# Gate, up and query projections with x held and the weights streamed, in a decode kernel on one core

## The chip, the cores and the metric

One NeuronCore of a Trainium2 chip runs the whole kernel. The metric is the device time of one execution in microseconds (us). Its five instruction queues are PE (TensorE; matmuls, with weight loads shown apart as PEld), DVE (VectorE), ACT (ScalarE), POOL (GpSimd) and SP (SyncE, which here issues every DMA). Matmuls write to PSUM, which is 8 banks of 128 partitions x 512 float32 values.

## What is computed

Two layers, each an attention block over a long cache and then a gated feed-forward, for a batch of 4 with one new token each (D = 512, 32 query heads, 8 key heads, 8192 cached positions, head size 128, F = 1792, all bfloat16). The same weights and caches serve both layers.

```python
def _A_ref(x, k_cache, v_cache, wq, wo):       # k_cache, v_cache: [4, 8, 8192, 128]
    q = (x @ wq).reshape(B, Sq, Hq, Dh).transpose(0, 2, 1, 3)
    k = jnp.repeat(k_cache, rep, axis=1)       # rep = 4
    v = jnp.repeat(v_cache, rep, axis=1)
    scores = jnp.einsum("bhqd,bhkd->bhqk", q, k) * (Dh ** -0.5)
    p = _softmax(scores, axis=-1)
    o = jnp.einsum("bhqk,bhkd->bhqd", p, v)
    return o.transpose(0, 2, 1, 3).reshape(B, Sq, Hq * Dh) @ wo

def _B_ref(x, w_gate, w_up, w_down):
    return (_silu(x @ w_gate) * (x @ w_up)) @ w_down

x = A_x
x = x + _A_ref(_layernorm(x), ...); x = x + _B_ref(_layernorm(x), ...)
x = x + _A_ref(_layernorm(x), ...); x = x + _B_ref(_layernorm(x), ...)
```

The caches are 128 MiB in all and are read almost wholly twice; that is nearly all the kernel's traffic.

## The kernel before

**Units.** The work is cut into 16 units, each a pair of key heads (`gp`, 0 to 3) and a batch element (`b`). A unit's K and its V are 4 MiB each. Layer 0 takes the units from 0 to 15, layer 1 takes 15, 14, 13, 12 and then 0 to 11, so that what lies in SBUF at the end of layer 0 can be used again.

**Slots and loads.** SBUF has four slots of 4 MiB and a fifth, `QS`, which first holds `wq`. The list `cmds` fixes the order of all loads: K and V of the units, the four parts of `wo`, at each layer's end the weights of the feed-forward (`W`: gate, up and the first parts of down; `W+`, `Wp`, `W0` to `W2`: the other parts of down). `pump` issues the next load on SP as soon as its place is free; `freed`, called as the program is written out, marks a place as free, and the issue then waits on semaphores for the last reader. Late in layer 1 a load is issued some 40 us before it lands.

**Scores and values.** K arrives with positions in partitions. VectorE transposes it in place, 32x32 blocks of 4-byte pairs (`turn`, L558). `scores` (L582) multiplies by `zq`, a stationary operand in which the unit's scaled queries stand in otherwise zero columns; GpSimd fills it for each unit from `qr` (`place_q`, L572), and VectorE does so for the first unit of a layer. The maximum of a unit (L588, L593, L596), the exponentials (L629), the transposes of the weights into `pT` (L646) and the products with V (`values`, L718, four 32-column quarters of the array at once) follow as an order written out by hand: `blocks` is the queue of PE work, `line` a queue of small steps that are let in between. The results of a unit are gathered (L766, L770), summed over partitions (L775) and scaled into `oT` (L780).

**After a group of heads.** When the four units of a `gp` are done, `close_group` lets `mix` (L801, L805) regroup the heads of `oT` so that they suit the layout of `wo`, and `rows` (L836) or, for the last group, `project` (L861) multiplies by `wo`. In both layers `mix` runs for the first two groups together, for the third and for the fourth by itself.

**Layer norm.** `center` (L884 to L898) subtracts the mean and squares; `deviation` (L903 to L907) gets 1/sqrt(variance) as `rstd`, which is multiplied in after the projection.

**Queries.** `qproj` (L917) holds 128x128 pieces of `wq` and moves the 4 columns of `xn`: 4 row blocks of D times 32 heads, 128 matmuls. The result has the head's 128 elements in partitions. VectorE multiplies by `rstd` into `qT` (L926), 16 matmuls with pieces of the identity (L936) spread it over partitions in the order that `scores` needs, and VectorE writes the first unit's `zq` (L572) and the copy `qr` for the others (L941). In layer 1 each eighth of `wq` is freed after its last matmul, for K.

**Feed-forward.** `ffn` (L961) does gate and up in the same way: 14 columns of F times 4 row blocks of D, 56 matmuls each. After the first, second and third row block of gate, places are freed for the last parts of down in layer 0. `rstd` is asked for after the second row block. Then come silu and the product (L975 to L982) into `hT`. The down projection is L999 in layer 0, with the weights held; in layer 1 `hT` is held and the weights move, in four quarters (L989). The final steps are two copies on VectorE (L1064) and two on ScalarE (L1062) and one store. Between the last matmuls of attention in layer 1 stand some matmuls that only keep PE busy (`stream`, L698). Two parts of `x_rows` (L879) add x itself into the result.

**The weights' layout.** With weights held, a piece of 128 columns is read with a stride of 2 or 4 (`columns`, `base`), because `w_down` lies in SBUF so that a partition holds `e` neighbouring rows of it; the third number in `WDS` is `e`.

## Time and profile before

| | us |
|---|---|
| median of 3 runs (644.95 to 645.78) | 645.25 |
| the profiled execution | 645.21 |
| its span, first to last instruction | 643.4 |

| engine | busy us | share of the span | instructions |
|---|---|---|---|
| PE matmuls | 416.7 | 65% | 3126 |
| PE weight loads | 180.0 | 28% | 3128 |
| VectorE | 421.7 | 66% | 593 |
| ScalarE | 42.3 | 7% | 118 |
| GpSimd | 11.6 | 2% | 44 |

271.8 MB pass the DMA engines at a mean of 422 GB/s. The mean granted clock of TensorE is 0.83 of full speed; it changes between 1.0 and 0.5 many times. The parts that the change touches:

| group | count | busy us | mean ns of one |
|---|---|---|---|
| L917 queries, matmul 128x4 | 256 | 7.5 | 166 |
| L961 gate and up, matmul 128x4 | 224 | 7.0 | 168 |
| L936 spreading the queries, matmul | 32 | 0.8 | 241 |
| L801 mix, matmul | 96 | 2.5 | 208 |
| L926, L941 queries on VectorE | 4 | 1.4 | 353 |
| L975 to L982 silu and product on VectorE and ScalarE | 14 | 3.6 | 258 |

Matmuls overlap in the array, so the busy time of a group is less than its count times the mean. "Idle before, releaser" in a row names what the engine waited for. Line numbers (L961) are those of the kernel before.

### The profile page before, as it was taken

What the parts mean: (1) busy time and instruction counts of PE and PEld (TensorE: products, weight loads), DVE (VectorE), ACT (ScalarE), POOL (GpSimd) and SP (SyncE); (2) the same over time, 40 slices, a digit from 0 to 9 for tenths busy, and PEclk for the clock granted to TensorE, in tenths of its full rate; (3) what the DMA queues carried; (4) which work ended last, traced back from release to release, by engine and by line L of the source; (5) the groups of instructions that cost most, each with busy time, mean ns of one, the idle gap of its engine ahead of it and who ended that gap; (6) DMA issues with size and microseconds to landing.
All of it is one profiled execution on the core that took longest, in us unless ns stands there. A gap on an engine that the chain in (4) does not pass through costs nothing.

```text
span 643.4 us, 7434 instructions
## 1 busy us (share of the span) xinstructions
PE 416.7 (65%) x3126; PEld 180.0 (28%) x3128; DVE 421.7 (66%) x593; ACT 42.3 (7%) x118; POOL 11.6 (2%) x44
## 2 busy tenths in 40 slices
PE   0673376456765757757866977776555577557877
PEld 0421122112222322222226432332221232222324
DVE  5275467455776656776952688887765567755964
ACT  0000000000000000000010110000000000000110
POOL 0000000000000000000000000000000000000000
PEclk9995786698877889766975899999778887769877
DMA  9999999999999999999999999999999999999996
GB/s 372 442 424 416 430 444 426 431 424 429 438 436 423 428 433 439 426 426 431 440 406 380 416 431 431 436 429 425 432 435 432 427 430 438 429 428 429 440 408 257
DMA packets 15872, 271.79 MB, mean 422 GB/s; under 512 B 1624, under 2 KB 1632, under 8 KB 7264
## 3 DMA queue, kind: packets, MB, share of 16 engines
q1 hardware_dynamic: 15840, 271.33, 99.0%
q8 instruction: 24, 0.39, 0.2%
q14 instruction: 8, 0.07, 0.0%
HBM read 271.32 MB, written 0.00 MB: 422 GB/s over the span
## 4 chain that ended last, share of the span: by engine, by line
DMA 61%; DVE 19%; PE 15%; issue 3%; another core or an unknown queue 1%; SPq 0%; DVEq 0%
DMA kvf<-in_A_k_cache_dram 49%; DVE kvf L558 15%; DMA kvf<-in_A_v_cache_dram 11%; PE ps L582 9%; PE ps L718 2%; DVE pb L770 2%; DMA kvf<-in_B_w_down_dram 1%; PE ps L961 1%; PE ps L917 1%; DVE pb L766 0%; DVE pT L646 0%; DVE scr L780 0%; SPq L93 0%; PE ps L861 0%
## 5 line engine op out<-in xcount | busy, mean ns | idle before, releaser
L582 PE MATMUL ps<-kvf,zq 128*128 128x512 bf16 x1024 | 292.9, 432 | 183.5 <-DVE kvf L558 178.8
L558 DVE STREAM_TRANSPOSE kvf<-kvf 128x2048 f32<-128x2048 f32 (+1 forms) x133 | 280.5, 2132 | 128.4 <-DMA kvf<-in_A_k_cache_dram 128.0
L582 PEld LDWEIGHTS ps<-kvf,zq 128*128 128x128 bf16 x1024 | 99.1, 108 | 340.2 <-DVE kvf L558 222.6
L718 PE MATMUL ps<-kvf,pT 128*32 128x512 bf16 x960 | 67.6, 405 | 1.1 <-DVE pT L646 1.1
L629 ACT ACTIVATE pb<-ps,tiny 128x512 bf16<-128x512 f32 x32 | 22.0, 687 | 525.9 <-DVE tiny L627 505.1
L646 DVE STREAM_TRANSPOSE pT<-pb 64x512 bf16<-64x512 bf16 x60 | 41.2, 686 | 2.7 <-ACT pb L629 1.7
L770 DVE SCALAR_TENSOR_TENSOR pb<-ps,tiny,pb 128x128 f32<-128x128 f32 x104 | 36.5, 351 | 4.7 <-PE ps L718 0.8
L588 DVE TENSOR_REDUCE tiny<-ps 128x1 f32<-128x512 f32 x32 | 22.0, 687 | 20.1 <-PE ps L582 20.1
L718 PEld LDWEIGHTS ps<-kvf,pT 128*32 128x32 bf16 x960 | 21.0, 99 | 31.2 <-issue 16.0
L775 PEld LDWEIGHTS ps<-sel,pb 128*128 128x128 f32 x64 | 17.0, 273 | 16.5 <-DVE pb L770 8.3
L572 POOL TENSOR_TENSOR zq<-scr,tiny 128x64 bf16<-128x64 bf16 x30 | 9.0, 299 | 527.1 <-PE ps L582 527.1
L596 DVE TENSOR_REDUCE mrm<-ps 1x8 f32<-1x128 f32 x32 | 8.8, 275 | 13.6 <-PE ps L593 13.6
L775 PE MATMUL ps<-sel,pb 128*128 128x8 f32 x64 | 12.4, 267 | 5.8 <-DVE pb L770 5.8
L619 PEld LDWEIGHTS ps<-mrm,tiny 128*128 128x128 f32 x60 | 13.0, 223 | 9.2 <-DVE scr L780 3.2
L917 PE MATMUL ps<-xn,kvf 128*128 128x4 bf16 x256 | 7.5, 166 | 11.5 <-DMA kvf<-in_A_wq_dram 11.2
L766 DVE TENSOR_SCALAR pb<-ps,tiny 128x128 f32<-128x128 f32 x32 | 10.1, 315 | 3.0 <-PE ps L718 3.0
L619 PE MATMUL ps<-mrm,tiny 128*128 128x16 f32 x60 | 9.9, 241 | 3.1 <-ACT mrm L631 3.1
L836 PE MATMUL ps<-wo_sb,scr 128*4 128x512 bf16 x48 | 11.0, 379 | 0.5 <-DVE scr L805 0.5
L917 PEld LDWEIGHTS ps<-xn,kvf 128*128 128x128 bf16 x256 | 7.3, 105 | 11.8 <-DMA kvf<-in_A_wq_dram 11.4
L631 ACT ACTIVATE mrm<-head,tiny 128x8 f32<-128x8 f32 x32 | 9.6, 301 | 1.0
L593 PE MATMUL ps<-identf,tiny 128*1 128x128 f32 x32 | 8.7, 273 | 0.7 <-DVE tiny L588 0.7
L790 DVE TENSOR_TENSOR xT<-xT,ps 128x16 f32<-128x16 f32 x6 | 1.0, 171 | 10.4 <-PE ps L846 4.7
(87 smaller groups left out, 120.3 us busy)
## 6 DMA issues: line engine op xcount, KB each, us to landing
kvf<-in_A_k_cache_dram SPq DMA_DIRECT2D x27, 4096.0 KB, 31.2
kvf<-in_A_v_cache_dram SPq DMA_DIRECT2D x27, 4096.0 KB, 33.9
kvf<-in_A_v_cache_dram SPq DMA_DIRECT2D x3, 2048.0 KB, 25.2
kvf<-in_A_k_cache_dram SPq DMA_DIRECT2D x9, 512.0 KB, 7.9
kvf<-in_A_k_cache_dram SPq DMA_DIRECT2D x2, 2048.0 KB, 9.4
kvf<-in_A_wq_dram SPq DMA_DIRECT2D x2, 2048.0 KB, 18.1
wo_sb<-in_A_wo_dram SPq DMA_DIRECT2D x4, 1024.0 KB, 41.4
kvf<-in_B_w_gate_dram SPq DMA_DIRECT2D x2, 1792.0 KB, 23.9
```

The costliest lines, as they stand in the source:

```text
L558: T.op("dve", lambda e: e.transpose(w, w), reads=names, writes=names)
L582: T.op("pe", lambda e: e.matmul(bank(bk)[:, 0:SW], lhsT=zq[:, z0:z0 + P], rhs=w[:, :, c // 2, :, c % 2], start=(q == 0 and c == 0), stop=( ...
L588: T.op("dve", lambda e: e.tensor_reduce(mx[:], bank(bk)[:, 0:SW], AX.X, ALU.max), reads=[f"pb{bk}"], writes=["mx"])
L619: T.op("pe", lambda e: e.matmul(at, lhsT=ones, rhs=mrm[:, i * H2:(i + 2) * H2], start=True, stop=True), reads=[f"m8{i}", "rsm", "onesf"], ...
L629: T.op("act", lambda e: e.activation(pb[:], bank(bk)[:, 0:SW], ACTF.Exp, bias=nm, accum_out=rs), reads=[f"pb{bk}", "nm"], writes=PB + ["rs"])
L646: T.op("dve", lambda e: e.transpose(dst, pb[hp]), reads=["pb", "row"], writes=[name])
L718: T.op("pe", lambda e: e.matmul(bank(k)[j * QB:(j + 1) * QB, q0 * Dh:q1 * Dh], lhsT=p_t[:, t, h, :], rhs=v[:, q0:q1, t, :], start=((last o ...
L766: T.op("dve", lambda e: e.tensor_scalar(into, o, own[:, q:q + 1], None, op0=ALU.mult), reads=[f"pb{k}", "own"], writes=["row"] if last els ...
L770: T.op("dve", lambda e: e.scalar_tensor_tensor(into, o, own[:, q:q + 1], into, op0=ALU.mult, op1=ALU.add), reads=[f"pb{k}", "own", iname], ...
L775: T.op("pe", lambda e: e.matmul(at, lhsT=into, rhs=sel[:], start=True, stop=True), reads=[iname, "sel"], writes=[name])
L836: T.op("pe", lambda e: e.matmul(bank(OUTB)[0:B, 0:D], lhsT=oT[:, h, :], rhs=wo_sb[:, h, :], start=(gp == groups[L][0] and r == 0), stop=(g ...
L917: T.op("pe", lambda e: e.matmul(at[:, h * B:(h + 1) * B], lhsT=wq_sb[:, kt, h * Dh:(h + 1) * Dh], rhs=xn[:, kt * B:(kt + 1) * B], start=(k ...
```

## The change

`qproj`, gate and up now hold the 4 columns of `xn` and move the weights. The output of a matmul is 4 partitions (the batch) by up to 512 columns. Four such matmuls, for four strips of columns, go to the four 32-column quarters of the array and so to partitions 0 to 3, 32 to 35, 64 to 67 and 96 to 99 of one bank. Gate and up have strips of 448 columns (`FW`), 16 matmuls each, and one strip of up is cut in two where its weights lie in two places. The queries have eight strips of 512 columns in two banks, 32 matmuls.

VectorE then transposes the bank in 32x32 blocks (`on_end`), which brings the columns back into partitions. For gate and up it is one transpose of 448 in place each, ahead of the same silu and product, whose operands now have the batch outside. Since a partition then holds 14 neighbouring rows of F, `w_down` is loaded so that each partition has 14 neighbouring rows too; in layer 1 its first two parts are runs of 8 and 4 KB instead of 2 KB.

For the queries there are two transposes of 512. In layer 0 both come before the first unit's `zq` is filled, in layer 1 only one of them does. `zq` is filled by two scaled copies on VectorE and two on ScalarE. Eight multiplications by `rstd`, of 32 partitions each, write `qr`. The 16 spreading matmuls, `qT` and L926, L936 and L941 go.

Two banks of PSUM are cleared once at the start, as the transposes read partitions that no matmul writes.

`mix` of layer 1 now takes the first three groups at once (`spot` gives a group's place in `oT` by its turn); in layer 0 it stays as it was. `deviation` uses another spare bank in `qproj`.

By the order of the instructions, no DMA issue changes its place on SP.

```diff
-        WDS = (((12, 14, 2), (10, 12, 2), (0, 2, 2), (2, 6, 4), (6, 10, 4)), ((0, 8, 2), (8, 12, 2), (12, 14, 2)))
+        WDS = (((12, 14), (10, 12), (0, 2), (2, 6), (6, 10)), ((0, 8), (8, 12), (12, 14)))
...
+        def wg_at(s, k, f, n):
+            o = s * SL + k * F + f
+            return kvf[:, o:o + n]
+
+        def wu_at(s, k, f, n):
             o = k * F + f
-            return columns((NSLOT + 1) * SL + o if o < RES else s * SL + O_WU + o - RES, e)
+            o = (NSLOT + 1) * SL + o if o < RES else s * SL + O_WU + o - RES
+            return kvf[:, o:o + n]
+
+        def strips(up, k):
+            for a in range(NA):
+                cuts = [a * FW, (a + 1) * FW]
+                if up and cuts[0] < RES - k * F < cuts[1]:
+                    cuts.insert(1, RES - k * F)
+                for f, end in zip(cuts, cuts[1:]):
+                    yield a, f, end - f
...
+        T.op("dve", lambda e: e.memset(ps[:, SBK[1] * BANKF:(OBK[0] + 1) * BANKF], 0.0),
+             writes=[f"pb{SBK[1]}", f"pb{OBK[0]}"])
...
+            a, b = WDS[L][j]
             o = 0 if w0 is pTf else wd_from(L, a)
-            T.dma("sp", w0[:, o:o + (b - a) * D].rearrange("p (m x) -> p m x", x=e_ * D),
-                  B_w_down[a * P:b * P, :].rearrange("(m p e) n -> p m (e n)", p=P, e=e_), sem_w["wd"][j],
+            T.dma("sp", w0[:, o:o + (b - a) * D], B_w_down.rearrange("(p f) n -> p (f n)", f=FO)[:, a * D:b * D], sem_w["wd"][j],
...
+            n = spot(L, gp)
+            if n < (1, 2)[L]:
                 return
-            gs = [0, 1] if gp == 1 else [gp]
-            line.append([0.5, None, lambda: mix(gs, fill)])
+            gs = groups[L][:n + 1] if n == (1, 2)[L] else [gp]
+            line.append([0.5, None, lambda: mix(L, gs, fill)])
...
+            gp, b = pair_gb(u)
+            first = gp // 2
+            W2 = REP * Dh
+            QK = (SBK[1], OBK[0])
+            assert W2 == BANKF and GP == 4 and QK[1] == QK[0] + 1
             for kt in range(KT):
                 if kt == KT // 2:
-                    deviation(lsc_sb, "lsc")
-                for h in range(Hq):
-                    q, last = 2 * kt + h * 2 // Hq, (h + 1) * 2 % Hq == 0
-                    T.op("pe", lambda e: e.matmul(at[:, h * B:(h + 1) * B],
-                                                  lhsT=wq_sb[:, kt, h * Dh:(h + 1) * Dh],
-                                                  rhs=xn[:, kt * B:(kt + 1) * B],
-                                                  start=(kt == 0 and h == 0), stop=(kt == KT - 1 and h == Hq - 1)),
-                         reads=[WQ[q], "xn"], writes=[name], sig=last)
-                    if L and last and q < NB - 2:
+                    deviation(lsc_sb, "lsc", SBK[0])
+                for k in ((first, 1 - first) if kt == KT - 1 else (0, 1)):
+                    q = 2 * kt + k
+                    for a in range(NA):
+                        f = ((2 * k + a % 2) * 2 + a // 2) * W2
+                        T.op("pe", lambda e: e.matmul(bank(QK[k])[a * QB:a * QB + B, :],
+                                                      lhsT=xn[:, kt * B:(kt + 1) * B], rhs=wq_sb[:, kt, f:f + W2], start=(kt == 0), stop=(kt == KT - 1)),
+                             reads=[WQ[q], "xn"], writes=[f"pb{QK[k]}"], sig=(a == NA - 1))
+                    if L and q < NB - 2:
                         if q == NB - 3:
                             T._wait("act", T._need((), [WQ[q]]))
                         freed(QS, q, q + 1)
-            T.op("dve", lambda e: e.tensor_tensor(qT, at.rearrange("p (h b) -> p b h", b=B),
-                                                  rstd[:].unsqueeze(2).to_broadcast([P, B, Hq]), ALU.mult),
-                 reads=[name, "rstd"], writes=["qT"] + OT)
-
-            pick = ident.rearrange("p (c j e) -> p c j e", c=2, e=2)
-            ob, oname = place("q", 0, NQR)
-            ob = ob.rearrange("p (c b g r) -> p c b g r", c=4, b=B, g=GP)
-            qv = qT.rearrange("p b (g h r) -> p b g h r", h=2, r=REP)
-            for c in range(4):
+
+            TO = (OBK[0], ONE)
+            assert TO[1] == TO[0] + 1 and TO[0] == QK[1]
+            ends = ps[:, TO[0] * BANKF:(TO[1] + 1) * BANKF].rearrange("p (k i r c) -> p k i r c", k=2, i=QB, r=REP)
+
+            def on_end(k):
+                src = bank(QK[k]).rearrange("p (x i e) -> p x e i", i=QB, e=2)
+                dst = bank(TO[k]).rearrange("p (i x e) -> p x e i", i=QB, e=2)
+                T.op("dve", lambda e: e.transpose(dst, src), reads=[f"pb{QK[k]}"], writes=[f"pb{TO[k]}"])
+
+            def place_first():
+                placed_q.add((L, u))
                 for a in range(NA):
-                    T.op("pe", lambda e: e.matmul(ob[a * QB:(a + 1) * QB, c],
-                                                  lhsT=pick[:, c // 2, :, c % 2],
-                                                  rhs=qv[:, :, :, a // 2, :], start=True, stop=True),
-                         reads=["qT", "ident"], writes=[oname], sig=(a == NA - 1))
-            place_q(L, u, "dve", ob, [oname])
-            T.op("dve", lambda e: e.tensor_copy(qr, ob), reads=[oname], writes=["qr", "made"])
+                    to = slice(a * QB, (a + 1) * QB)
+                    g = a // 2 * 2 + gp % 2
+                    of = slice(g * QB, (g + 1) * QB)
+                    dst = zd[to, :, a, 0:REP].rearrange("p c r -> p r c")
+                    src = ends[of, first, b]
+                    if a // 2:
+                        T.op("act", lambda e: e.activation(dst, src, ACTF.Copy, scale=rstd[of, b:b + 1]),
+                             reads=[f"pb{TO[first]}", "rstd"], writes=["zq1"])
+                    else:
+                        T.op("dve", lambda e: e.tensor_scalar(dst, src, rstd[of, b:b + 1], None, op0=ALU.mult),
+                             reads=[f"pb{TO[first]}", "rstd"], writes=["zq"])
+
+            on_end(1)
+            if first:
+                place_first()
+            on_end(0)
+            if not first:
+                place_first()
+            for a in range(NA):
+                to = slice(a * QB, (a + 1) * QB)
+                for h in range(2):
+                    g = a // 2 * 2 + h
+                    of = slice(g * QB, (g + 1) * QB)
+                    src = ends[of, :, 0:B].rearrange("p k b r c -> p k b (r c)")
+                    dst = qr[to, h].rearrange("p k b r c -> p k b (r c)")
+                    r2 = rstd[of].unsqueeze(1).unsqueeze(3).to_broadcast([QB, 2, B, 4 * REP])
+                    T.op("dve", lambda e: e.tensor_tensor(dst, src, r2, ALU.mult),
+                         reads=["rstd"], writes=["qr", "made"] + [f"pb{k}" for k in TO])
...
+            def on_end(k):
+                blk = bank(k)[:, 0:FW].rearrange("p (i f) -> p f i", f=FO)
+                T.op("dve", lambda e: e.transpose(blk, blk), reads=[f"pb{k}"], writes=[f"pb{k}"])
...
+                for kt in range(*ks):
+                    parts = list(strips(bk == ub, kt))
+                    for n, (a, f, w) in enumerate(parts):
+                        T.op("pe", lambda e: e.matmul(bank(bk)[a * QB:a * QB + B, f - a * FW:f - a * FW + w],
+                                                      lhsT=xn[:, kt * B:(kt + 1) * B], rhs=at(s, kt, f, w),
+                                                      start=(kt == 0), stop=(kt == KT - 1)),
                              reads=rooms[wname] + names[wname] + ["xn"], writes=[f"pb{bk}"],
-                             sig=(fo == FO - 1 and kt == ks[1] - 1))
+                             sig=(kt == ks[1] - 1 and n == len(parts) - 1))
...
+            on_end(gb)
             T.op("dve", lambda e: e.tensor_tensor(fb(gr), fb(gT), rb, ALU.mult),
...
+            on_end(ub)
+            T.op("dve", lambda e: e.tensor_tensor(hT.rearrange("p (f b) -> p b f", b=B), fb(eg), fb(uT), ALU.mult), reads=[f"pb{ub}", "eg"], writes=["hT"])
```

## Prediction

> **What bounds the kernel now.** I read the page first: DMA share and queues.
>
> ```profile
> span 643.4 us, 7434 instructions
> ...
> DMA  9999999999999999999999999999999999999996
> ...
> q1 hardware_dynamic: 15840, 271.33, 99.0%
> q8 instruction: 24, 0.39, 0.2%
> q14 instruction: 8, 0.07, 0.0%
> ```
>
> The 16 DMA engines are full in 39 of 40 slices; PE and VectorE are busy for two thirds. Faster matmuls bring nothing while the caches stream. Beside the data, a queue named "instruction" moves 24 packets of 16 KB: the kernel's own program.
>
> Second view, the chain of waits from 600 us:
>
> ```profile
> 585.97 43.37 DMA kvf<-in_A_v_cache_dram
> 629.33 0.04 issue
> 629.38 0.86 PE ps L718 x16
> ...
> 635.46 0.84 PE ps L961 x28
> 636.29 0.22 PE ps L903 x2
> 636.52 2.22 PE ps L961 x84
> 638.74 0.52 PE ps L879 x8
> 639.26 1.49 PE ps L989 x47
> 640.75 0.03 issue
> 640.78 0.42 PE ps L989 x8
> ```
>
> The last V load (landed 629.33, its last piece 630.61) releases 12 us of dependent work. Gate and up take 3.3 us of it.
>
> Third, busy time by stage:
>
> ```profile
> 634.00:636.00 2.00, 1.72 (x43) 1.25 (x40) 0.96 (x6) 0.00 (x0) 0.00 (x0) 1.00 1.02 376
> 636.00:638.00 2.00, 2.00 (x76) 2.00 (x74) 0.62 (x3) 0.81 (x3) 0.00 (x0) 0.69 0.64 240
> 638.00:640.00 2.00, 2.00 (x68) 1.69 (x65) 0.94 (x4) 0.00 (x0) 0.00 (x0) 0.50 0.22 86
> ```
>
> The last columns (granted clock, DMA share, GB/s) show that the DMA engines do not finish together: most are done by 636, a few work to 640.7. The trace's semaphore records show the spread: each transfer has 16 part-landings, one an engine. For the last V piece the first is at 625.65, the last at 630.61: 4.96 us apart; at 33 us the spread was 1.6. Each instruction packet (some 1.05 us long in the packet records) makes one engine later by about 1.5 us; the widest spread goes from 3.60 to 4.92 just after the 21st, at 583.48. The landing that everything waits for is that of the engine hit most often.
>
> Fourth, the timeline of VectorE between the layers:
>
> ```profile
> 356.60 0.29 DVE L926 TENSOR_TENSOR scr<-ps,tiny 128x128 bf16<-128x128 f32 x1 [3.67 <-PE ps L917]
> 357.43 0.23 DVE L572 TENSOR_TENSOR zq<-ps,tiny 128x64 bf16<-128x64 f32 x1 [0.53 <-PE ps L936]
> 357.57 0.41 DVE L941 CAST scr<-ps 128x256 bf16<-128x256 f32 x1
> 357.90 2.37 DVE L521 STREAM_TRANSPOSE kvf<-ps 128x1024 f32<-128x1024 f32 x2
> 360.19 5.59 DVE L558 STREAM_TRANSPOSE kvf<-kvf 128x2048 f32<-128x2048 f32 x3
> 366.12 0.69 DVE L588 TENSOR_REDUCE tiny<-ps 128x1 f32<-128x512 f32 x1 [0.34 <-PE ps L582]
> ```
>
> There VectorE has hardly a gap for 10 us.
>
> **The change part by part.** *Fewer PE instructions.* The queries fall from 128+16 to 32 matmuls a layer, gate and up from 112 to 33, the joined mix saves 16: 2x112 + 2x79 + 16 = 398, each with its weight load, 796 instructions. The page has 3126 + 3128 of them for 24 packets, about 260 a packet: three packets fewer. What counts is when they come. The 21st was fetched when PE stood at instruction 5338 (waits counted); by then 638 (796 less the last 158) have been saved, so it comes where the old kernel stood at 5976, at 635 us, after V has landed. The widest spread at V then stays near 3.6: V lands up to 1.35 us earlier. The bounds are 0 (another engine collects as many) and 1.35; I take 1.0, because of the layer boundary below.
>
> [...]
>
> *Gate and up in the last stage.* Matmuls in four quarters are priced by L718, 128x512: 16 in 0.98 us at full clock (61 ns each), 24 in 2.75 us at half clock (115). With 448 columns a projection is 16 x 54 = 0.86 us or 16 x 100 = 1.6, against 56 in 1.7. No row shows one with 4 stationary columns and 448 moving; L989 (4 columns, 128 moving, 31 ns) is nearest in kind, L836 (no quarters, 229 ns each) is the bound above. I take L718, its clock between.
> Gate ends 0.5 us earlier, but L975 also waits for rstd, and a transpose of 128x448 f32 comes first: L558 takes 1.215 us for 1024 and 2.294 for 2048, so 0.14 + 448 x 1.054 ns = 0.61 us. L975 starts at about 637.4 instead of 637.28. Its chain to L981 took 1.52 and ends at 638.9; the second transpose is queued behind it on VectorE: 0.62 with its gap, then the product, 0.22. hT is ready at 639.8 instead of 639.11: +0.7. The two transposes read and write PSUM in a strided order that no row has; from L646 (strided, 512 elements, 0.69) to twice that, hT is late by 0.7 to 1.5; below 0.4 it cannot be, for the ends are two instructions more in one chain.
>
> *Down.* L989 takes 1.86 us after hT where its weights are there. It waited for the last two pieces (landed 640.11 and 640.73). In layer 1 the first two are now runs of 8 and 4 KB in place of 2 KB; at 84 ns for 2 KB, 159 for 4 and 309 for 8 (packet records) an engine saves 8 x (4x84-309) + 8 x (2x84-159) = 0.29 us. But the 21st packet now falls on these weights, where the old 23rd and 24th fell: the slowest engine delivers them as late as before, at 640.73 - 0.29 = 640.44. So with V 1.0 earlier, hT comes at 638.8, PE alone would end at 640.8, and the last eight matmuls after the last piece end at about 640.85. Before, that was 641.16. Layer 0's pieces keep their sizes.
>
> *Sum.* -0.3 us by the slowest engine for the down weights; -0.6 if it is less late. I take -0.5: 645.21 (the profiled execution; span 643.4 and 1.8 around it) gives 644.7. The median before is 645.25, so nothing has to be shifted.
>
> *Layer boundary.* In layer 0 the end of FFN hangs on the down weights (the chain has 5.9 us of DMA up to 350.4), so hT 0.5 later is hidden; uncovered it would cost its 0.5. The queries at half clock: 32 x 115 = 3.7 against 3.6 us on PE, even. Then two transposes of 512 (0.68 each), two scaled copies (0.23; ScalarE does two more beside them) and eight products of 32x128, priced as L926, 0.29 each: 4.2 us of VectorE in place of 0.93. With the first transpose starting 0.4 earlier, L521 begins 2.6 us later; behind it are queued the transposes L558 and L588, for which PE's L593 and so the scores wait. Half of it goes in VectorE's gaps up to 370 us; the V load issued at 370.88 comes about 1.3 late. The quickest DMA engines have 0.4 us in hand there, and idle up to 0.9. The engines that end last are 1.3 to 2 us behind at that point and lose nothing; one that ends in the middle does. That is why I took 1.0 of 1.35.
> ScalarE's copy L1040 and GpSimd's clearing of pT come some 2 us later; their readers come at 370, so this costs 0 (at most those 2 us if a reader waited). No SP issue changes place.
>
> *Layer 0's start.* Clearing two banks (1 us, by L328 0.49 for 512) and the queries cost 0: VectorE is idle from 4 to 8 us, and the first load that waits for a score (issued 34.70) stands behind transfers that keep the engines fed to 54 us. Joining the mix moves 8 matmuls from one V step to another, under the stream: 0.
>
> **Rivals.** *Full relief* (0.25): the down weights' slowest engine is spared too, and PE keeps its full clock through L989 (the denser matmuls keep it busier; the clock fell at 636.74). For it: three packets fewer. Against: the 21st falls in the last stage. It gives 1.35 + 0.3 = -1.6: 643.6.
>
> *No relief* (0.17): which engine a packet meets is not in my hands, and another is 4.9 us late for V. Then the tail alone counts: +0.7 for hT, all of it shown on PE: 645.9. With the upper price of the transposes, 646.7.
> [...]
>
> *VectorE holds up the stream between the layers* (0.12): if the strided transposes and the eight small products cost twice what I take, L521 starts 6 us later and the V load of 370.88 is 4 us late. It decides once the lateness passes the 0.4 us in hand plus the 2 us by which the slowest engines lag; beyond that each microsecond counts. 4 - 2.4 = 1.6, with the tail's 0.3: 647.1, slower. Against: DMA share is 1.02 from 358 to 380.
>
> *The quarters do not run together* (0.03): at 229 ns a matmul gate and up take 33 x 0.2 = 6.6 us instead of 3.3, +3.3: 648.5. Against: L718 at 61 ns.
>
> **Numbers.** My case has 0.43, and 644.7. The range leaves out the worst of the last two and the best of the first: 643.4 to 646.6. 0.2% is 1.29 us, about what a measurement of this kernel can tell from no change. Faster by more is most of full relief and a little of mine: 0.28. Slower by more is the last two rivals and the dear transposes: 0.18. Within: 0.54.
>
> **What would show it.** 21 packets in the instruction queue; last V piece at about 629.5; L718's 61 to 115 ns in the new matmuls; transposes at 0.6 to 0.7; hT about 9.2 us after V's last piece instead of 8.5; PE waiting for the down weights at the end. A V piece still at 630.6, or DMA share under 0.95 between 370 and 380, would prove me wrong.

## The result: 1.3 us slower, and the profile after

| | before | changed |
|---|---|---|
| median of 17 runs, us | 645.25 | 646.59 |
| lowest to highest, us | 644.18 to 647.74 | 645.68 to 649.54 |
| profiled execution, us (span) | 645.21 (643.4) | 649.54 (647.7) |
| a second profiled execution, us (span) | | 646.38 (644.5) |

The ratio is 1.0028, 95% interval 1.0019 to 1.0037: slower, where the prediction had 644.7. The first profiled execution of the changed kernel lies 3 us above its median, so sizes are taken from the second too (the run `changed_again`), which is nearer to it.

First the page of the changed kernel:

```profile
span 647.7 us, 6670 instructions
...
q8 instruction: 21, 0.34, 0.2%
```

There are three instruction packets fewer, as predicted. What that is worth in time is tried below.

The chain of waits of the changed kernel, first where layer 1 begins, then from the last V load on:

```profile
357.86 9.97 PE ps L597 x32
...
588.36 43.80 DMA kvf<-in_A_v_cache_dram
632.21 0.86 PE ps L733 x16
...
644.39 1.10 PE ps L1039 x56
```

L597 are the scores (L582 before), L733 the products with V, L1039 the down projection (L989 before). The last V load lands at 632.16 and its last piece at 633.44; before it was 629.33 and 630.61. In the second profile the last piece lands at 630.87. So V is not 1.0 us earlier but 0.3 to 2.8 later, and the question is where in the run this begins. When the last V piece of layer 0 lands there is nothing yet: it does so at 337.03, before at 337.08.

Busy time by stage, the changed kernel; the columns are those of the prediction's third view, the last three granted clock, DMA share and GB/s:

```profile
370.00:372.00 2.00, 2.00 (x12) 0.91 (x11) 1.22 (x5) 0.08 (x1) 0.00 (x0) 1.00 0.94 307
...
374.00:376.00 2.00, 1.56 (x8) 0.55 (x7) 1.55 (x2) 0.00 (x0) 0.00 (x0) 1.00 0.88 352
...
378.00:380.00 2.00, 0.83 (x16) 0.21 (x8) 2.00 (x2) 0.00 (x0) 0.00 (x0) 1.00 0.87 352
```

This is the sign that the prediction named as proof against itself: between 370 and 380 us the DMA engines run dry. In the second profile it is weaker: of the five shares there only the last, 0.92, is under 0.95; before, the lowest is 0.96. The V load there is issued at 372.67 instead of 370.88 (372.81 in the second profile), and soon after it the first landing of each transfer is 2.4 us later (404.56 against 402.17, and at the last V piece 628.10 against 625.65); in the second profile it is 1.9 us later (404.05 and 627.54).

Not all of that arises at this V load. The K load that is issued at 351 first lands at 355.87 before, and at 356.36 and 357.03 in the two profiles of the changed kernel. So 0.5 and 1.2 us are there already, from the end of layer 0: there the last part of the down weights is issued at 345.04 and 345.82, before at 344.54. These 1.2 us need not cost time: the run `new_queries_mended_old_gate_up`, below, has 1.3 us of the same (357.18) and is as fast as the kernel before.

The two profiles of the changed kernel differ by 3.2 us, and at this V load the slowest DMA engine is already that far apart. The sixteen part-landings of the load, one an engine, end at 383.90 in the first profile and at 380.78 in the second, and lie 4.06 and 1.10 us apart; at the K load ahead of it they were 1.37 and 1.69 apart. What held that engine up in the first profile is not known.

What was late ahead of that issue? The timeline of VectorE in the changed kernel (L534 and L571 are the transposes L521 and L558 of before, L603 the maximum L588):

```profile
358.37 2.54 DVE L985 TENSOR_TENSOR scr<-ps,tiny 32x128 bf16<-32x128 f32 x8
360.94 2.38 DVE L534 STREAM_TRANSPOSE kvf<-ps 128x1024 f32<-128x1024 f32 x2
363.35 5.63 DVE L571 STREAM_TRANSPOSE kvf<-kvf 128x2048 f32<-128x2048 f32 x3
368.91 0.65 DVE L603 TENSOR_REDUCE tiny<-ps 128x1 f32<-128x512 f32 x1
```

The new work on VectorE, which ends with the eight products, puts L534 3.04 us back, a little more than the 2.6 of the prediction. The maximum L603 comes 2.79 us later than before (366.12). That is one candidate. The other is in PE's timeline, changed kernel and then kernel before:

```profile
354.64 1.88 PE L939 MATMUL ps<-kvf,xn 128*4 128x512 bf16 x16
357.86 9.96 PE L597 MATMUL ps<-kvf,zq 128*128 128x512 bf16 x32 [1.34 <-ACT zq L965]
```

```profile
356.95 0.41 PE L936 MATMUL ps<-scr,identf 128*32 128x64 bf16 x16 [0.38 <-DVE scr L926]
357.71 8.38 PE L582 MATMUL ps<-kvf,zq 128*128 128x512 bf16 x32 [0.35 <-DVE zq L572]
```

The same 32 matmuls start 0.15 us later and take 1.6 us longer. Before them PE stands still for 1.34 us, waiting for `zq`; before the change it stood still for 0.38 and 0.35 with work in between. The granted clock is the third column from the right in the stages, here for the changed kernel and then for the kernel before:

```profile
360.00:362.00 2.00, 2.00 (x6) 0.67 (x5) 1.90 (x4) 0.00 (x0) 0.00 (x0) 0.50 0.99 414
362.00:364.00 2.00, 2.00 (x7) 0.72 (x6) 1.97 (x3) 0.00 (x0) 0.00 (x0) 0.58 1.00 413
```

```profile
360.00:362.00 2.00, 2.00 (x10) 0.78 (x8) 2.00 (x2) 0.00 (x0) 0.00 (x0) 0.93 1.00 416
```

The clock goes from 0.5 to 1.0 at 363.66, before at 360.26; in the second profile at 362.46. Among these matmuls of 512 columns one starts 0.43 us after the other at the half clock and 0.22 at the full one (the 9.96 us for 32 hold both).

### The profile page after: what moved, and what is told of

The parts are those of the page before. It is cut to its first block, busy times and chain, and to the rows that moved or that the text cites. A ratio compares the mean times of both kernels' runs of the same rounds, so it can differ in the third digit from the quotient of the medians.

```text
span 647.7 us, 6670 instructions
## 1 busy us (share of the span) xinstructions
PE 415.9 (64%) x2730; PEld 168.8 (26%) x2730; DVE 431.9 (67%) x615; ACT 43.6 (7%) x122; POOL 11.8 (2%) x44
## 4 chain that ended last, share of the span: by engine, by line
DMA 59%; DVE 22%; PE 13%; issue 4%; ACT 0%; SPq 0%; ACTq 0%; POOL 0%; DVEq 0%; POOLq 0%
DMA kvf<-in_A_k_cache_dram 45%; DVE kvf L571 16%; DMA kvf<-in_A_v_cache_dram 11%; PE ps L597 7%; DMA kvf<-in_A_wq_dram 3%; DVE pb L785 2%; PE ps L733 2%; DMA kvf<-in_B_w_down_dram 1%; PE ps L939 1%; DVE pb L781 1%; DVE pT L661 1%; PE ps L1010 1%; DVE ps L537 0%; DVE scr L795 0%; DVE ps L954 0%
## 5 line engine op out<-in xcount | busy, mean ns | idle before, releaser
L597 PE MATMUL ps<-kvf,zq 128*128 128x512 bf16 x1024 | 292.7, 432 | 186.9 <-DVE kvf L571 178.1
L571 DVE STREAM_TRANSPOSE kvf<-kvf 128x2048 f32<-128x2048 f32 (+1 forms) x133 | 280.5, 2132 | 121.7 <-DMA kvf<-in_A_k_cache_dram 121.5
L597 PEld LDWEIGHTS ps<-kvf,zq 128*128 128x128 bf16 x1024 | 98.9, 108 | 346.2 <-DVE kvf L571 223.0
L733 PE MATMUL ps<-kvf,pT 128*32 128x512 bf16 x960 | 67.0, 402 | 1.3 <-DVE pT L661 1.3
L603 DVE TENSOR_REDUCE tiny<-ps 128x1 f32<-128x512 f32 x32 | 22.0, 688 | 21.9 <-PE ps L597 21.9
L733 PEld LDWEIGHTS ps<-kvf,pT 128*32 128x32 bf16 x960 | 20.9, 98 | 31.5 <-issue 16.4
L939 PE MATMUL ps<-kvf,xn 128*4 128x512 bf16 x64 | 7.5, 620 | 11.1 <-DMA kvf<-in_A_wq_dram 10.8
L954 DVE STREAM_TRANSPOSE ps<-ps 128x512 f32<-128x512 f32 x4 | 2.9, 732 | 9.0 <-PE ps L939 9.0
L733 PE MATMUL ps<-kvf 128*32 128x512 bf16 (+2 forms) x96 | 5.5, 363 | 4.2 <-DMA kvf<-in_A_v_cache_dram 4.0
```

The costliest lines, as they stand in the source:

```text
L571: T.op("dve", lambda e: e.transpose(w, w), reads=names, writes=names)
L597: T.op("pe", lambda e: e.matmul(bank(bk)[:, 0:SW], lhsT=zq[:, z0:z0 + P], rhs=w[:, :, c // 2, :, c % 2], start=(q == 0 and c == 0), stop=( ...
L603: T.op("dve", lambda e: e.tensor_reduce(mx[:], bank(bk)[:, 0:SW], AX.X, ALU.max), reads=[f"pb{bk}"], writes=["mx"])
L733: T.op("pe", lambda e: e.matmul(bank(k)[j * QB:(j + 1) * QB, q0 * Dh:q1 * Dh], lhsT=p_t[:, t, h, :], rhs=v[:, q0:q1, t, :], start=((last o ...
L939: T.op("pe", lambda e: e.matmul(bank(QK[k])[a * QB:a * QB + B, :], lhsT=xn[:, kt * B:(kt + 1) * B], rhs=wq_sb[:, kt, f:f + W2], start=(kt ...
```

## The experiments

Three theories. CLOCK: the scores run longer at the half clock, so the loads that they release come late and the DMA engines run dry. VECTORE: the queue of products on VectorE does that. LAST STAGE (called TAIL in the first texts): gate and up after the last V piece cost the time. Diffs are against the kernel that is named.

### Halves of the change

`gate_up_only` is the kernel before with the new gate, up and down layout; `queries_only` has the new queries and mix. Against the changed kernel, each puts back what belongs to the other half; of that, the calls:

```diff
+            T.op("dve", lambda e: e.tensor_tensor(qT, ...))        # gate_up_only: qproj, place_q, mix and groups as before
...
+                for fo in range(FO):                               # queries_only: ffn, load_wd and WDS as before
+                    f = base(L, fo)
```

> The kernel before with gate, up and the layout of the down weights changed; the queries and the mix as before. CLOCK theory (the loss is made between the layers: after the new queries PE waits 1.3 us for zq, its granted clock comes up 3.2 us later, the scores end 1.7 us later, the loads that they release come 1.8 us later and the DMA engines run dry): the boundary is as before, scores ending near 366.1 and the V load at 370.9, and the time is 645.0 to 645.7, ratio 0.999 to 1.001. TAIL theory (the two transposes and the lower clock of gate and up in the last stage cost the time): 646.5 to 647, ratio 1.002 to 1.003, with the last V piece at 630.6 as before.

> The kernel before with the queries and the mix changed; gate, up and the down weights as before. CLOCK theory and VECTORE theory (eight small products ahead of the hold-back transposes make VectorE late): the whole loss is here, scores ending near 367.8, the V load 1.8 us later than 370.9, time 646.3 to 647, ratio 1.0015 to 1.003. TAIL theory: 645.0 to 645.6, ratio 0.999 to 1.001.

Measured: 1.0028 (1.0014 to 1.0043) and 1.0032 (1.0021 to 1.0044). Each half alone costs as much as both together, so the halves do not add. That would fit a common step into which both run; it does not prove one. In both profiles the scores end late (368.24 and 368.04, before 366.09) and the V load comes at 373.04 and 372.89. For `queries_only`, that is what CLOCK and VECTORE expected. For `gate_up_only` LAST STAGE had the time, but no theory had the late scores: its queries and its VectorE queue are those of before. Its PE timeline shows why the scores are late:

```profile
356.99 0.29 PE L946 MATMUL ps<-scr,identf 128*32 128x64 bf16 x5 [0.38 <-DVE scr L936]
357.86 0.35 PE L946 MATMUL ps<-scr,identf 128*32 128x64 bf16 x11 [0.58 <-issue]
358.55 9.69 PE L592 MATMUL ps<-kvf,zq 128*128 128x512 bf16 x32 [0.34 <-DVE zq L582]
```

Among the 16 matmuls that turn the queries (L936 before) PE stops for 0.58 us after the fifth, and "issue" means that it waits for nothing that the profile shows. The scores start 0.84 us later, and again the clock comes up later (363.80, before 360.26).

Next, gate and up in one layer only; `ffn_new` is the changed function beside the old one:

```diff
-            ffn(L)
+            (ffn_new if L == 1 else ffn)(L)        # gate_up_layer1_only; L == 0 in gate_up_layer0_only
```

> The kernel before with the new gate, up and down layout in layer 1 alone. LAST STAGE theory: the boundary is untouched (V load 370.9, last V piece 630.6), hT comes 9.8 to 10.4 us behind V instead of 8.5, the down weights no longer end last: time 645.7 to 646.4, ratio 1.001 to 1.002. If gate/up alone lost its 1.8 us at the boundary: 645.0, ratio 1.000.

> The kernel before with the new gate, up and down layout in layer 0 alone. LAST STAGE theory: the last stage is as before and nothing is lost, 644.8 to 645.3, ratio 0.999 to 1.001. BOUNDARY theory of gate/up (fewer instructions move the packets, PE is held up at 357 and its clock comes up a step later): scores end near 368 instead of 366.1, 645.8 to 646.5, ratio 1.001 to 1.0025.

Measured: layer 1 only 1.0007 (0.9999 to 1.0016), layer 0 only 1.0026 (1.0017 to 1.0035). So most of the loss of gate and up does not arise in the last stage, where the prediction had looked for it, but by the layer in which the same work is hidden. In `gate_up_layer0_only` PE stops at the same matmul, for 0.77 us, and the V load comes at 373.01.

### The edge of an instruction packet

In both kernels PE stops at the same count of its instructions: the traces have 3225 matmuls and weight loads ahead of the stop. If a packet ends there, other instructions ahead of it move the stop. `pad(n)` puts n matmuls of 4 columns, whose result nobody reads, into a V step of layer 0, at 172 us. A matmul has a weight load beside it: 79 are the 158 instructions that the new gate and up save in layer 0, and 49 are 98, which with 158 make 256, near the prediction's count of about 260 to a packet. `three_packets_more`, below, bears it out: 768 more, 3 x 256, are three packets more on its page.

```diff
 def values(L, u):
     gp, b = pair_gb(u)
+    pad(79 if (L, u) == (0, 6) else 0)        # gate_up_only_shifted; 49 in before_shifted
```

> The run gate_up_only with 79 idle matmuls of 4 columns (158 PE instructions with their weight loads) early in layer 0's stream, so that the instruction packets fall at layer 1's queries as they do in the kernel before. PACKET EDGE theory (in gate_up_only PE runs out of instructions for 0.6 to 0.8 us at the sixth of the 16 matmuls that turn the queries, the scores start 0.7 us late and the clock comes up 3.4 us later): the stall is gone, the scores end near 366, the V load comes near 371, time 645.0 to 645.8, ratio 0.999 to 1.001. If gate/up loses by its own work: 646.4 to 647, as gate_up_only.

> The kernel before with 49 such idle matmuls (98 PE instructions) early in layer 0's stream and nothing else, so that a packet's edge falls at the sixth of the 16 matmuls that turn the queries of layer 1. PACKET EDGE theory: PE stalls 0.6 to 0.8 us there, the scores start 0.7 us late, the V load comes at 372 to 373, time 646.3 to 647, ratio 1.0015 to 1.003, though only 0.3 us of work is added, under the stream. Otherwise: 645.1, ratio 0.9995 to 1.0005.

The timelines of PE, `gate_up_only_shifted` and then `before_shifted`:

```profile
357.20 0.41 PE L952 MATMUL ps<-scr,identf 128*32 128x64 bf16 x16 [0.38 <-DVE scr L942]
```

```profile
357.11 0.29 PE L942 MATMUL ps<-scr,identf 128*32 128x64 bf16 x5 [0.38 <-DVE scr L932]
357.62 0.36 PE L942 MATMUL ps<-scr,identf 128*32 128x64 bf16 x11 [0.22 <-issue]
358.31 9.77 PE L582 MATMUL ps<-kvf,zq 128*128 128x512 bf16 x32 [0.33 <-DVE zq L572]
```

The stop goes from the one and comes to the other, after the fifth matmul, where it was to come; there the trace has 3481 matmuls and weight loads ahead of it, 256 more than above. `before_shifted` has nothing of the change, only 49 idle matmuls (1.4 us) 185 us earlier, and is 1.0030 (1.0019 to 1.0040): as slow as the changed kernel. Its stop is short (0.22 us where 0.6 to 0.8 were expected), but the clock comes up at 363.71 and the V load at 372.87. That so short a stop is the whole way to the 1.9 us is not shown. `gate_up_only_shifted` has 1.0016 (1.0005 to 1.0028) where `gate_up_only` had 1.0028 (1.0014 to 1.0043); its V load comes at 371.32. That is less of a loss, though more than the 1.001 that was expected at most, but the intervals overlap, and what is left was not taken apart.

Three more packets elsewhere cost nothing that can be told here (`three_packets_more`, below: 1.0010 beside 1.0007). The stop at this place, in the hand-over from queries to scores, was 0.2 to 0.8 us long, and the measured time of `before_shifted` is 1.9 us longer.

### The boundary mended

Changed kernel, the products moved to ScalarE (GpSimd's mask `quadr` carries `rstd`):

```diff
-                    T.op("dve", lambda e: e.tensor_tensor(dst, src, r2, ALU.mult), ...)
+                    T.op("act", lambda e: e.activation(dst, src, ACTF.Copy), ...)
```

> The changed kernel with the eight products of 32x128 taken from VectorE: ScalarE copies them unscaled, behind its copy of pT, and GpSimd's masks carry rstd. VECTORE theory: the hold-back transposes start near 358.4 instead of 360.9, the V load comes near 371, time near 645, ratio to before 0.999 to 1.001. CLOCK theory: the transposes start 2.5 us earlier too, but the scores still end near 367.8 and the V load comes near 372.5: 646.3 to 647, ratio 1.0015 to 1.003.

Changed kernel, PE kept busy before the scores of layer 1:

```diff
+            if L:
+                for _ in range(3):
+                    T.op("pe", lambda e: e.matmul(bank(SBK[0]), lhsT=wo_sb[:, 0, 0:P], rhs=wo_sb[:, 0, :], start=True, stop=True), ...)
```

> The changed kernel with three idle matmuls of 128x512 on PE after layer 1's queries, in the 1.3 us in which it waited for zq. CLOCK theory: PE's granted clock rises near 360 instead of 363, the scores end near 366.2 instead of 367.8, the V load comes near 371 to 371.5 (VectorE, still 3 us late, may now hold it), time 645.0 to 645.8, ratio 0.999 to 1.001. VECTORE theory and TAIL theory: nothing changes, 646.3 to 647, ratio 1.0015 to 1.003.

Measured: 1.0009 (0.9999 to 1.0018) and 1.0023 (1.0014 to 1.0032). By the times, both are what VECTORE expected and neither is what CLOCK expected: with the products off VectorE 0.0019 of the 0.0028 is gone, though PE still stands still for 1.56 us ahead of the scores, and with PE kept busy hardly anything is gone. The PE timeline of `pe_kept_busy` says more:

```profile
356.49 1.25 PE L949 MATMUL ps<-wo_sb 128*128 128x512 bf16 x3
357.89 7.13 PE L597 MATMUL ps<-kvf,zq 128*128 128x512 bf16 x32 [0.15 <-ACT zq L970]
...
369.66 0.27 PE L608 MATMUL ps<-identf,tiny 128*1 128x128 f32 x1 [1.99 <-DVE tiny L603]
```

The clock is up at 357.4 and the scores take 7.13 us instead of 9.96, as the first half of CLOCK has it. But then PE waits 1.99 us for the maximum L603, which stands on VectorE behind the products and L571. L603 comes at 368.95, as in the changed kernel (368.91), where the scores ended so late that PE hardly had to wait for it. PE's clock falls again from 371.05 to 374.47, and the V load comes at 373.38. So VectorE's queue is a second limit, less than a microsecond behind the first. In the second profile of the changed kernel it is already the later one, by half a microsecond:

```profile
369.37 0.65 DVE L603 TENSOR_REDUCE tiny<-ps 128x1 f32<-128x512 f32 x1
371.38 0.38 PE L639 MATMUL ps<-mrm,tiny 1*128 1x8 f32 x2 [0.17 <-DVE mrm L611]
```

One profile of `products_on_scalar` does not tell the two apart, for the clock happened to come up at 356.62, ahead of the gap. So it was profiled once more.

> The run products_on_scalar once more, for a second profile: there the clock came up at 356.6, before the gap, so its one profile does not tell VectorE from the clock. CLOCK theory: where the clock comes up at 361 to 364 in this execution, the scores end after 367 and the V load comes after 372, although VectorE's queue is empty, and the time is 646 or more; where it comes up by 360, V load by 371 and the time 645 to 646. VECTORE theory: V load by 371.2 in either case.

Measured: 645.22 us, clock up at 362.04, scores to 367.05, V load at 371.90. These are neither theory's numbers: the V load follows the scores by 4.85 us, as CLOCK says, but at 371.90 the time is still that of the kernel before. So this kernel's median gain on the changed one, the clearest that a single mend has, is VECTORE's, and CLOCK does not explain it.

VectorE's queue by itself, on the kernel before:

```diff
-            T.op("dve", lambda e: e.tensor_copy(qr, ob), ...)
+            for _ in range(7 if L else 1):
+                T.op("dve", lambda e: e.tensor_copy(qr, ob), ...)
```

> The kernel before, with layer 1's copy of the queries (128x256, 0.41 us) made seven times over: 2.5 us more of VectorE ahead of the hold-back transposes, as in the change, and nothing else. CLOCK theory: the scores still run from 357.7 to 366.1, the largest-score reduction comes 2.2 us late and holds PE by some 0.6 us, V load 371 to 371.6, time 645.1 to 645.9, ratio 1.000 to 1.0015. VECTORE theory (the queue alone makes the loss): V load 372.5 or later, 646.3 to 647, ratio 1.0015 to 1.003.

Measured: 0.9999 (0.9990 to 1.0007). 2.8 us more on VectorE cost nothing, and the maximum is as late as in the changed kernel:

```profile
368.84 0.65 DVE L588 TENSOR_REDUCE tiny<-ps 128x1 f32<-128x512 f32 x1
```

So a late queue on VectorE by itself is not enough in the kernel before. The profiled execution is the slowest of its 11 (646.24, median 645.25): in it the clock came up late, at 363.46, and the V load at 372.65, though PE does the work of the kernel before.

Then both mends together: on the changed kernel, on one with the old gate and up, and on one with them old in layer 1 alone:

```diff
-            ffn(L)
+            (ffn_old if L else ffn)(L)        # mended_old_last_stage
```

> The changed kernel with both mends of the boundary: the eight products on ScalarE and three idle matmuls on PE behind the queries. If lateness between the layers (PE's clock first, VectorE's queue behind it) and the longer last stage are the two losses: the scores run from 358 to 365.2, max_p follows at once and the V load comes near 370, the last V piece lands at 629.5 to 630.5, hT still 9.8 us or more behind it; time 645.0 to 645.7, ratio 0.999 to 1.001. If the boundary were the whole loss: 643.9 to 644.6.

> The kernel before with the new queries and mix, their products on ScalarE and the three idle matmuls; gate, up and down as before. If the two losses are the boundary and the last stage, neither is here: V load near 370, last V piece near 630, hT 8.5 us behind it, time 643.9 to 644.9, ratio 0.998 to 1.000. If the new queries lose by something else: 646 or more.

> The run boundary_mended with gate, up and the down layout of layer 1 as before (new in layer 0 alone): the version that should be best if the boundary costs 1.2 us and the new last stage about 0.4: hT 8.5 us behind the last V piece, time 644.6 to 645.3, ratio 0.998 to 1.0005. If the new last stage costs nothing: 645.5, as boundary_mended.

Measured: 1.0007 (0.9998 to 1.0015); 1.0002 (0.9993 to 1.0010); and, with the new gate and up in layer 0 alone, 1.0006 (0.9997 to 1.0014). `boundary_mended` in PE's timeline:

```profile
358.43 7.34 PE L598 MATMUL ps<-kvf,zq 128*128 128x512 bf16 x32
```

So 0.0021 of the change's 0.0028 goes with the boundary, 1.35 us, and the two intervals do not overlap. The new last stage costs nothing that these runs can tell (1.0007 against 1.0006; a loss of up to some 0.8 us would not show). None of them beats the kernel before; nor does that kernel with two idle matmuls in its own gaps there, one behind the queries and one behind L936:

```diff
+            idle()
             T.op("dve", lambda e: e.tensor_tensor(qT, ...))
...
+            idle()
             place_q(L, u, "dve", ob, [oname])
```

> The kernel before with two idle matmuls of 128x512 in PE's gaps between layer 1's queries and scores. CLOCK theory: the clock comes up by 360.3 at the latest, often by 357, the scores end at 365 to 366.1, V load 369.8 to 370.9. Since the DMA engines are fed there already, the time moves little: 644.6 to 645.3, ratio 0.998 to 1.0005; a version that may beat both.

Measured: 1.0005 (0.9994 to 1.0016), clock up at 362.19 in the profile, though PE was kept busy and CLOCK expected 360.3 at the latest; the V load at 371.95.

### The V load alone

Is the late V load enough, with no engine's work changed? The first try only wrote `finished` down two blocks later:

```diff
-                finished(K(L, u), q, q + 1)
+                late_end.append(q)
+                while late_end and (len(late_end) > 2 or q == NB - 1):
+                    i = late_end.pop(0)
+                    finished(K(L, u), i, i + 1)        # for the second pair of layer 1
```

> The kernel before, with the loads that the second pair's keys of layer 1 release issued two blocks of scores (about 1.75 us) later; no instruction of PE or VectorE changes. DMA theory (the loss is that the V load comes after the quickest DMA engines have run dry): V load near 372.6 instead of 370.9, the first landing of the last V piece 1 to 2 us later than 625.65, time 646.2 to 647, ratio 1.0015 to 1.003. If the lag of the slower engines covered it, as the prediction had it: 645.0 to 645.4, ratio 0.9995 to 1.001.

Every engine's order and waits came out as in the kernel before, and the V load at 370.80. It says nothing of the theory. It is the kernel before a second time, and its 0.9989 (0.9980 to 0.9999) shows that 0.001 between two kernels is not yet a difference. The second try holds SyncE:

```diff
+                        T._wait("sp", T._need([f"pb{SBK[turn_of[u]]}"], ()))
                         finished(K(L, u), i, i + 1)
```

> The kernel before, with SyncE held before the loads that the second pair's keys of layer 1 release until PE has done two more blocks of scores (the run v_load_late moved only the order in which they were written down, and the V load came at 370.8). DMA theory: V load near 372.6, the first landing of the last V piece 0.8 to 2 us later than 625.65, time 646 to 647 beside 645.2, ratio 1.001 to 1.003. If the lag of the slower engines covers it: ratio 0.999 to 1.0005.

Measured: 1.0015 (1.0006 to 1.0024). In the profile the V load comes at 373.92, later than meant, since the clock came up late too (362.53), and the first landing of the last V piece at 628.71, 3.06 later than before. Its busy time by stage:

```profile
372.00:374.00 2.00, 2.00 (x11) 0.86 (x9) 1.93 (x4) 0.41 (x3) 0.00 (x0) 1.00 0.81 332
374.00:376.00 2.00, 1.56 (x7) 0.40 (x5) 1.00 (x1) 0.00 (x0) 0.00 (x0) 1.00 0.62 143
```

The DMA engines run dry for over a microsecond, and the time follows, though by less (1.0 us): the engines that lag may take up a part. With the prediction's cover of 0.4 + 2 us, 0.6 of the 3.04 us of this profile would be left to lose; the interval goes from 0.4 to 1.5 us, so this run does not settle how much the lag covers. It does show that a late V load alone costs time.

### All profiles in one table

Each run left one profile. "Scores" is when the first pair's scores of layer 1 end, "V load" when the load is issued, "first" the first landing of the last V piece. Ordered by the V load:

| kernel | clock up | scores | V load | first | this execution, us |
|---|---|---|---|---|---|
| `three_packets_more` | 356.11 | 365.24 | 370.10 | 626.16 | 645.07 |
| `new_queries_mended_old_gate_up` | 356.55 | 365.26 | 370.12 | 626.90 | 645.84 |
| `mended_old_last_stage` | 358.79 | 365.51 | 370.37 | 625.75 | 643.99 |
| `products_on_scalar` | 356.62 | 365.67 | 370.52 | 626.79 | 645.78 |
| `boundary_mended` | 358.93 | 365.77 | 370.63 | 626.35 | 645.28 |
| `v_load_late` | 360.15 | 366.00 | 370.80 | 625.86 | 644.27 |
| before | 360.26 | 366.09 | 370.88 | 625.65 | 645.21 |
| `gate_up_only_shifted` | 360.90 | 366.53 | 371.32 | 626.20 | 646.76 |
| `gate_up_layer1_only` | 361.33 | 366.64 | 371.43 | 626.43 | 643.84 |
| `products_again` | 362.04 | 367.05 | 371.90 | 626.67 | 645.22 |
| `before_kept_busy` | 362.19 | 367.15 | 371.95 | 626.68 | 645.21 |
| `vector_late` | 363.46 | 367.85 | 372.65 | 628.25 | 646.24 |
| changed | 363.66 | 367.81 | 372.67 | 628.10 | 649.54 |
| `changed_again` | 362.46 | 367.46 | 372.81 | 627.54 | 646.38 |
| `before_shifted` | 363.71 | 368.08 | 372.87 | 628.00 | 646.83 |
| `queries_only` | 363.97 | 368.04 | 372.89 | 627.64 | 646.74 |
| `gate_up_layer0_only` | 363.09 | 368.22 | 373.01 | 627.97 | 647.54 |
| `gate_up_only` | 363.80 | 368.24 | 373.04 | 628.17 | 647.67 |
| `pe_kept_busy` | 357.40 | 365.02 | 373.38 | 628.03 | 648.03 |
| `v_load_held` | 362.53 | 367.29 | 373.92 | 628.71 | 646.99 |

In 17 of 20 the V load is 4.79 to 4.86 us behind the scores. In the 18th, `changed_again`, it is 5.35, and in `pe_kept_busy` 8.36: there VectorE's queue came last. The twentieth is `v_load_held`, where it was held. Up to 371.95 the last V piece begins to land by 626.90 and the 11 executions average 645.13 (643.84 to 646.76); from 372.65 on it begins at 627.54 or later, and the 9 average 647.33 (646.24 to 649.54). If there is a step, it lies near 372. The groups overlap (`gate_up_only_shifted` has 646.76, `vector_late` 646.24), and each row is one execution.

The clock column also shows where the clock came up. Moved by whole steps of 3.41 us (in the changed kernel the changes at 336.36 and 363.66 are eight of them apart) into one such stretch, 13 of the 20 fall between 359.5 and 360.9, one at 361.3 and six between 362.0 and 362.5. So the place differs from execution to execution, but one place is the most frequent. Near it the kernel before comes up at 360.26, while `vector_late`, whose step would have been at 360.05 and whose scores start 0.38 us later than in the kernel before, comes up a whole step later.

> The changed kernel once more, for a second profile of it: CLOCK theory expects the granted clock to come up at 363 to 364 again and the V load at 372.4 to 373; where the clock comes up by 360.5 in this execution, VECTORE theory still expects a V load after 372, CLOCK theory one by 371.5. Time 645.7 to 647.5.

`changed_again` (646.38) had the clock at 362.46, a little earlier than CLOCK expected, and the V load at 372.81 as expected.

### Instruction packets and the last V piece

On `boundary_mended`, 768 more PE instructions as idle matmuls:

```diff
+    pad((0 if not 1 <= u <= 8 else 32) if not L else 16 if 5 <= order[1].index(u) < 13 else 0)
```

> The run boundary_mended with 384 idle matmuls of 4 columns (768 PE instructions, three packets of 256) in eight V steps of each layer, away from the boundary and the last stage, so that the edges elsewhere stay where they were: 24 packets in place of 21. The prediction's term (three packets fewer bring V 1.0 us earlier, bounds 0 and 1.35): 646.0 to 646.9, ratio 1.001 to 1.003. If packets cost the last V piece little: 645.3 to 645.8, as boundary_mended.

The page counts 24 packets, and the ratio is 1.0010 (1.0001 to 1.0019) beside 1.0007 without them. The prediction's 1.0 us for three packets is not there (0.2 us, uncertain by about 0.8). The spread of the 16 part-landings at the last V piece is 3.25 us with 24 packets here, 3.81 with 21 in `boundary_mended`; in the kernel before and the same program a second time it is 4.96 and 3.46, in the changed kernel 5.34 and 3.33.

## Why the prediction was wrong, step by step

- **The layer boundary** is the step that failed. The prediction let it cost only a part of the gain at V: "the V load issued at 370.88 comes about 1.3 late", and the engines that end last "are 1.3 to 2 us behind at that point and lose nothing". It came 1.8 to 1.9 late, and the time was lost: mending the boundary brings 1.35 us back. The work on VectorE was sized well (4.2 us predicted; 0.73 + 0.59 + 0.73 + 2.54 = 4.59 measured), and its queue is one of the two limits. The other was missed. "The queries ... on PE, even" left out that PE then waits 1.34 us for `zq`, and that a clock which comes up later makes the scores end later: by 1.72 and 1.37 us in the two profiles, of which 0.15 and 0.61 are a later start. The profile of before showed where to look: the clock of 0.50 until 360, the 0.35 and 0.38 us of waiting, the 8.38 us of scores. The place is shown by the mends. How the 1.35 us divide between the clock and VectorE is not.
- **Fewer PE instructions**: the count was right (21), the term of 1.0 us mis-sized: `three_packets_more` has 0.2 us, which cannot be told from zero. It rested on the spread of one execution, 4.96 us, which was a wide one. What the smaller count did do, in the half `gate_up_only`, was to bring a stop of PE, 0.58 us, into the hand-over from queries to scores.
- **Gate and up in the last stage**: the prices held (eight matmuls 0.92 us at the half clock, the transposes 0.66 and 0.67, the product 0.28). The sum did not: `hT` comes 10.9 and 10.3 us after the last V piece in the changed kernel, 9.2 predicted, 8.5 before. Gate did not end 0.5 us earlier, since the clock fell at 633.31 and 635.53, before at 636.74. Where it held to 636.51 (`products_on_scalar`), the way from gate's first matmul to `hT` is 4.59 us against 3.65, +0.9 where +0.7 was predicted. In the second profile this stage carries most of the difference from the profile of before: the last V piece is 0.26 us later, `hT` 2.07, the whole execution 1.17. But that V piece of before was late itself; in the same program a second time (`v_load_late`) it landed at 629.32. The ratios of `gate_up_layer1_only` and of the mends put the cost of this stage at little or nothing.
- **Down**: PE does not wait for the down weights. They land at 643.41, `hT` is ready at 644.33, and 56 matmuls take 1.10 us with the clock up again since 643.55 (in the second profile 640.87 and 641.18).
- **Layer 0**: right as far as it can be told. Its stream ends as before (last V piece 337.03), and its down projection starts as before (L1049 at 350.33, L999 before at 350.49). The 0.5 and 1.2 us by which the next K loads first land later were not foreseen; no run shows that they cost time. Joining the mix was not tried alone; with the mended queries it costs nothing (1.0002).
- **The rivals**: the result lies nearest to "VectorE holds up the stream between the layers", by place and sign. Its two conditions were not met: the transposes and products cost what the prediction took, not twice that, and the V load was 1.8 to 1.9 us late, not more than 0.4 + 2. The time was lost all the same. It is also the rival that names one of the two limits (`products_on_scalar`, `pe_kept_busy`), though the same lateness cost the kernel before nothing (`vector_late`).

By how much the clock came up later is seen in the two traces: in the changed kernel the change down at 336.36 and the change up at 363.66 are 27.30 us apart, 8 x 3.41; before, 336.37 and 360.26 are 23.89 us apart, 7 x 3.41. A gap of 1.34 us in PE went with a step at which the clock stayed at the half, and so did, in `before_shifted`, two shorter gaps (0.38 and 0.33 us) and a stop of 0.22.

**What stays open.** Where the clock steps fall differs from execution to execution, and only profiled ones show it, so how often each kernel meets the late step is not known. That is why the clock's part is seen in single profiles only. The two limits were not told apart: `products_on_scalar` gains more than CLOCK explains, and `vector_late` loses less than VECTORE expects. That the stop of PE is the fetch of instructions is argued from its place, which moved by the 256 that were counted. And the late V load alone (`v_load_held`) accounts for 1.0 us, not surely for the whole loss.

## What to carry to other kernels

Where a stream of loads is released by compute, look at what the releasing engine's clock does just there: a short wait in front of a long run of matmuls can go with a clock that comes up later (here 1.34 us ahead of 32 matmuls, and the clock up at 363.66 instead of 360.26). Then look for the engine that is just behind: the mend of one limit showed little here while the second was less than a microsecond away (`pe_kept_busy`: 1.0023 beside 1.0028). A change of the number of instructions can move a stop of PE: here 98 more of them, 185 us earlier, went with one of 0.22 us in the hand-over. Run such a change once more with some idle instructions put in early, before the work itself is blamed. And do not size a term by the spread of one execution: profile the same kernel twice.

## What the runs showed that was not expected

- 49 idle matmuls of 4 columns, under the stream and 185 us before the place where they mattered, made the kernel before 1.9 us slower (1.0030).
- 384 such matmuls elsewhere cost nothing that can be told (1.0010 against 1.0007).
- In the profiles of the kernel before and of the changed one, with 49 and 51 changes, the granted clock changes only at whole multiples of 3.413 us from its other changes (within 0.01 us), and with the same work on PE up to there it came up at 360.15, 360.26, 361.33, 362.53 and 363.46 in five executions (`v_load_late`, before, `gate_up_layer1_only`, `v_load_held`, `vector_late`).
